# Retention attention with a gated feed-forward layer: moving the v loads from GpSimd's queue to the hardware queues, with the first tiles put in a new order

## The chip, the cores and the metric

The kernel runs on one core of one Trainium2 chip. The metric is the device time of one execution in microseconds; the kernel before takes 238.09 us (median of 3 runs, 238.08 to 238.14). The profiled execution took 238.38 us, of which 236.7 us lie between its first and its last instruction; times inside the profile are counted from that first instruction.

## The reference, cut to what matters

Attention with a decaying state (batch 4, 8 heads, 768 positions, 64 numbers per head), then a feed-forward layer on 3072 tokens with 512 features and 1536 hidden units:

```python
gamma = 1.0 - 2.0 ** (-5.0 - np.arange(H))
for t in range(S):                       # the state decays by gamma, then takes k v^T
    state = gamma * state + einsum('bhd,bhe->bhde', k[:, :, t], v[:, :, t])
    y[:, :, t] = scale * einsum('bhd,bhde->bhe', q[:, :, t], state)
x = y.transpose(0, 2, 1, 3).reshape(B * S, H * D)
gate = 1 / (1 + exp(-(x @ w_gate)))
out = (gate * (x @ w_val)) @ w_out
```

## The kernel before, where the change touches it

The 3072 tokens are cut into 24 chunks of 128 (index `g`) and into 6 token tiles of 512 (index `t`, four chunks each). For a chunk the kernel loads k, q and v. k and q are turned into bf16 during the transfer[...]; v stays in 32 bits, and it too is issued by GpSimd, except that of chunk 0.

```python
def load_v(g, eng):
    vf[g] = ld.tile([C, H, D], F32, tag="vf", name="vf", bufs=8)
    eng.dma_start(out=vf[g], in_=src(v, g))

def load_kq(g):                       # k and q of a chunk, cast to bf16 on the way
    ...
    nc.gpsimd.dma_start(out=kn[g], in_=src(k, g))
    nc.gpsimd.dma_start(out=qn[g], in_=src(q, g))

def load_chunk(g):
    load_kq(g)
    load_v(g, nc.gpsimd)
```

The steps of one chunk: `transposes(g)` turns k and q on TensorE and ScalarE copies them out (`qkT`); from chunk 12 on a DMA transpose does it. `scale_v` multiplies v by the decay table into `vs`. `scores` makes k q^T, `masks` applies the causal mask on VectorE. `inter` adds the part of the output that comes from the state, `state` adds k v^T to the state, `intra` the part from inside the chunk, `state_out` copies the state out on ScalarE, and `y_out` multiplies by the table `taby` on VectorE into `xT`, the input of the feed-forward layer.

The feed-forward layer of a token tile is 12 groups `up(t, n1)` (gate and value, 8 matmuls; ScalarE applies the sigmoid, VectorE multiplies) and 8 half groups `down` (6 matmuls each; after every second one ScalarE copies the result out). The three weights are loaded by GpSimd in pieces: six of gate and of value (`load_gate_val`, two `n1` each) and four of the output weight (`load_out`, three `n1` each).

The start, before the loop over the tiles. `keep_on(n)` issues n matmuls whose result nobody uses; they fill TensorE's waits:

```python
    scale_v(0, nc.gpsimd)
    load_gate_val(0)
    scale_v(1, nc.gpsimd)
    load_chunk(3)
    load_gate_val(1)
    load_gate_val(2)
    ...                               # chunk 0's k and q cast on VectorE and ScalarE
    keep_on(36)
    transposes(0)
    make_taby(slice(256, 384))
    extend_taby()                     # GpSimd: taby[384:768] from taby[0:384]
    for s in range(3, NFF // 2):
        load_gate_val(s)
    load_chunk(4)
    for s in range(4):
        load_out(s)
    for g in range(5, 8):
        load_chunk(g)
    ...                               # chunks 0, 1 and 2, with keep_on between
    intra(2)
    y_out(2)
    scale_v(3, nc.vector)
    keep_on(8)
    up(0, 0, 0, 384)                  # the columns of chunks 0 to 2 only
    up(0, 1, 0, 384)
    transposes(3)
    scores(3)
    masks(3)
    inter(3); state(3); state_out(3)
    up(0, 2, 0, 384)
    intra(3)
    y_out(3)
    up(0, 3, 0, 384)
    up_columns(0, range(4), 384, 512) # chunk 3's columns of the first four groups
```

In the loop the steps of the next tile's chunks are put between the groups. For tile 0 they are:

```python
        if t == 0:
            groups = groups[4:]
            steps = [lambda: step_t(4), lambda: step_s(4), lambda: step_y(4), lambda: step_t(5), lambda: step_s(5),
                     lambda: step_t(6), lambda: step_y(5, 6), lambda: step_t(7), lambda: step_y(6, 7)]
            place = [4, 5, 7, 9, 10, 11, 12, 13, 14]
```

`step_t` is transposes and `scale_v`; `step_s` scores and masks; `step_y(g, n)` is inter, scores of chunk n, state, intra, masks of n and `y_out`. Chunk 7's last step comes in tile 1, after the first group there.

Of the kernel before, what the change touches and what calls it, by code (L numbers as in the profile page):

```python
# [9 lines left out]
F32 = mybir.dt.float32  # L10
BF16 = mybir.dt.bfloat16
I32 = mybir.dt.int32
AX = mybir.ActivationFunctionType
ALU = mybir.AluOpType
# [3 lines left out]
def kernel(  # L18
# [10 lines left out]
    nc = tc.nc  # L29
# [28 lines left out]
        return x[b, :, c * C:(c + 1) * C, :].rearrange("h s d -> s h d")  # L58

    def load_v(g, eng):  # L60
        vf[g] = ld.tile([C, H, D], F32, tag="vf", name="vf", bufs=8)
        eng.dma_start(out=vf[g], in_=src(v, g))  # L62

    def load_kq(g):
        kn[g] = ld.tile([C, H, D], BF16, tag="kn", name="kn")
        qn[g] = ld.tile([C, H, D], BF16, tag="qn", name="qn")
        nc.gpsimd.dma_start(out=kn[g], in_=src(k, g))  # L67
        nc.gpsimd.dma_start(out=qn[g], in_=src(q, g))  # L68

    def load_chunk(g):  # L70
        load_kq(g)
        load_v(g, nc.gpsimd)

    wg = wpool.tile([128, KT, D_FF], BF16, name="wg")
    wv = wpool.tile([128, KT, D_FF], BF16, name="wv")
# [2 lines left out]
    def load_gate_val(s):  # L78
        cols = slice(s * 256, (s + 1) * 256)
        for dst, w in ((wg, moe_w_gate), (wv, moe_w_val)):  # L80
            nc.gpsimd.dma_start(out=dst[:, :, cols],  # L81
                                in_=w.rearrange("(kk p) n -> p kk n", p=128)[:, :, cols])

    def load_out(s):
# [7 lines left out]
    nc.sync.dma_start(out=qf, in_=src(q, 0))  # L92
    nc.scalar.preload_act_table(AX.Exp)
    load_v(0, nc.sync)
    tokv = const.tile([128, NCH], I32, name="tokv")
    nc.gpsimd.iota(tokv, pattern=[[C, NCH]], base=0, channel_multiplier=1)
    ident = const.tile([128, 128], BF16, name="ident")
    make_identity(nc, ident)
    toky = const.tile([128, 384], I32, name="toky")
    nc.gpsimd.iota(toky, pattern=[[1, 384]], base=0, channel_multiplier=0)  # L100
    load_chunk(1)
    causal = const.tile([128, 128], F32, name="causal")
    nc.gpsimd.memset(causal, 1.0)
    nc.gpsimd.affine_select(causal, causal, pattern=[[1, 128]], base=0, channel_multiplier=-1,
                            compare_op=ALU.is_ge, fill=0.0)
    load_chunk(2)

    tabv = const.tile([128, NCH, H], F32, name="tabv")
    for h in range(H):
# [16 lines left out]
        for p in range(NP):  # L126
            nc.scalar.activation(taby[:, p, cols], toky[:, cols], AX.Exp, scale=lgp[:, p:p + 1], bias=lsc)

    def extend_taby():
        nc.gpsimd.tensor_tensor(taby[:, :, 384:768], taby[:, :, 0:384],  # L130
                                gup.unsqueeze(2).to_broadcast([128, NP, 384]), op=ALU.mult)

    causal4 = causal.unsqueeze(1).to_broadcast([128, NP, 128])

# [7 lines left out]
    def transposes(g):  # L142
        tp = pa.tile([128, 2 * NP, C], BF16, tag="tp", name="tp")
        for i, x in enumerate((kn[g], qn[g])):
            for p in range(NP):
                nc.tensor.transpose(tp[:, i * NP + p, :], pair(x, p), ident)  # L146
        qkT[g] = at.tile([128, 2 * NP, C], BF16, tag="qkT", name="qkT", bufs=3)
        nc.scalar.activation(qkT[g], tp, AX.Copy)  # L148
# [7 lines left out]
    def scale_v(g, eng):  # L156
        vs[g] = ld.tile([C, H, D], BF16, tag="vs", name="vs", bufs=4)
        eng.tensor_tensor(vs[g], vf[g], tabv[:, g % NCH, :].unsqueeze(2).to_broadcast([C, H, D]),  # L158
                          op=ALU.mult)
# [16 lines left out]
    def inter(g):  # L176
        y[g] = pa.tile([128, NP, C], F32, tag="y", name="y")
        if g % NCH > 0:
            for p in range(NP):
                nc.tensor.matmul(y[g][:, p, :], zbd[(g - 1) % 2][:, p, :], qkT[g][:, NP + p, :],  # L180
                                 start=(p == 0), stop=False, skip_group_check=True)

    def state(g):
        b, c = divmod(g, NCH)
        if c == 0:
            zps[b] = pa.tile([128, NP, D], F32, tag="z", name="z", padded_shape=[128, NP, C])
        if c < NCH - 1:
            for p in range(NP):
                for i in range(2):
                    nc.tensor.matmul(zps[b][i * D:(i + 1) * D, p, :], kn[g][:, 2 * p + i, :], vs[g][:, 2 * p + i, :],  # L190
                                     start=(c == 0 and p == 0), stop=True, skip_group_check=True)

    def state_out(g):
        b, c = divmod(g, NCH)
        if c < NCH - 1:
            for i in range(2):
                half = slice(i * D, (i + 1) * D)
                nc.scalar.copy(zbd[g % 2][half, :, half], zps[b][half])  # L198
# [8 lines left out]
    def y_out(g):  # L207
        c = g % NCH
        if g % 4 == 0:
            xT[g // 4] = at.tile([128, NP, 512], BF16, tag="xT", name="xT")  # L210
        col = (g % 4) * C
        nc.vector.tensor_tensor(xT[g // 4][:, :, col:col + C], y[g], taby[:, :, c * C:(c + 1) * C], op=ALU.mult)  # L212

    def step_t(g):
        if g < XBAR:
            transposes(g)
        scale_v(g, nc.vector if g < XBAR else nc.gpsimd)

    def step_s(g):
        scores(g)  # L220
        masks(g)

    def step_y(g, nxt=None):
        inter(g)
        if nxt is not None:
            scores(nxt)
        state(g)
        intra(g)
        state_out(g)
        if nxt is not None:  # L230
            masks(nxt)
        y_out(g)
# [10 lines left out]
    def up(t, n1, lo=0, hi=512):  # L243
        if t not in hT:
            hT[t] = ffn.tile([128, NFF, 512], BF16, tag="hT", name="hT", bufs=2)
        ps = []
        for w in (wg, wv):
            u = pf.tile([128, 512], F32, tag="ff", name="ff")
            for kk in range(KT):
                nc.tensor.matmul(u[:, lo:hi], w[:, kk, n1 * 128:(n1 + 1) * 128], xT[t][:, kk, lo:hi],  # L250
                                 start=(kk == 0), stop=(kk == KT - 1))
            ps.append(u)
        gs = ffn.tile([128, 512], F32, tag="gs", name="gs")
        nc.scalar.activation(gs[:, lo:hi], ps[0][:, lo:hi], AX.Sigmoid)  # L254
        nc.vector.tensor_tensor(hT[t][:, n1, lo:hi], gs[:, lo:hi], ps[1][:, lo:hi], op=ALU.mult)  # L255
# [34 lines left out]
    def keep_on(n):  # L290
        u = pf.tile([128, 512], F32, tag="ff", name="ff")
        for _ in range(n):
            nc.tensor.matmul(u[:, :128], ident, ident, start=True, stop=True)  # L293
# [18 lines left out]
                eng.dma_start(out=out[row:row + 128, first:first + 128], in_=ob)  # L312


    scale_v(0, nc.gpsimd)
    load_gate_val(0)
    scale_v(1, nc.gpsimd)
    load_chunk(3)
    load_gate_val(1)
    load_gate_val(2)  # L320
    make_taby(slice(0, 256))
    kn[0] = ld.tile([C, H, D], BF16, tag="kn", name="kn")
    qn[0] = ld.tile([C, H, D], BF16, tag="qn", name="qn")
    nc.vector.tensor_copy(kn[0], kf)
    nc.scalar.copy(qn[0], qf)
    keep_on(36)
    transposes(0)
    make_taby(slice(256, 384))
    extend_taby()
    for s in range(3, NFF // 2):  # L330
        load_gate_val(s)
    load_chunk(4)
    for s in range(4):
        load_out(s)
    for g in range(5, 8):
        load_chunk(g)
    keep_on(8)
    scores(0)
    masks(0)
    keep_on(8)  # L340
    transposes(1)
    inter(0)
    state(0)
    state_out(0)
    intra(0)
    y_out(0)
    keep_on(8)
    scores(1)
    masks(1)
    keep_on(4)  # L350
    inter(1)
    state(1)
    state_out(1)
    transposes(2)
    nc.scalar.preload_act_table(AX.Sigmoid)
    intra(1)
    y_out(1)
    scale_v(2, nc.vector)
    keep_on(12)
    scores(2)  # L360
    masks(2)
    inter(2)
    state(2)
    state_out(2)
    keep_on(10)
    intra(2)
    y_out(2)
    scale_v(3, nc.vector)
    keep_on(8)
    up(0, 0, 0, 384)  # L370
    up(0, 1, 0, 384)
    transposes(3)
    scores(3)
    masks(3)
    inter(3)
    state(3)
    state_out(3)
    up(0, 2, 0, 384)
    intra(3)
    y_out(3)  # L380
    up(0, 3, 0, 384)
    up_columns(0, range(4), 384, 512)


    def ups(t):
# [5 lines left out]
    for t in range(NT):  # L391
        groups, steps, place = ups(t) + downs(t), [], []
        if t == NT - 1:
            groups[-2:] = [lambda: last_down(t)]
        if t == 0:
            groups = groups[4:]
            steps = [lambda: step_t(4), lambda: step_s(4), lambda: step_y(4), lambda: step_t(5), lambda: step_s(5),
                     lambda: step_t(6), lambda: step_y(5, 6), lambda: step_t(7), lambda: step_y(6, 7)]
            place = [4, 5, 7, 9, 10, 11, 12, 13, 14]
        elif t + 1 < NT:  # L400
            steps = attention(t + 1)
            place = [0, 1, 3, 5, 7, 8, 10, 13, 17]
        if t == 1:
            groups[:2] = [lambda: up(1, 0, 0, 384), lambda: step_y(7), lambda: up(1, 1, 0, 384),
                          lambda: up_columns(1, range(2), 384, 512)]
            place = [p + 2 for p in place]
        if t + 2 < NT:
            for g in range(4 * t + 8, 4 * t + 12):
                load_chunk(g)
        for i, group in enumerate(groups):  # L410
            if i == len(groups) - 9:
                for g in range(4 * t + 8, 4 * t + 12):
                    if XBAR <= g < NG:
                        xbar(g)
            group()
            for p, step in zip(place, steps):
                if p == i:
                    step()
# [30 lines left out]
```

## Time and profile before

| | value |
|---|---|
| device time, median | 238.09 us |
| span in the profile | 236.7 us |
| granted TensorE clock | 0.997 |
| TensorE busy | 227.0 us (96%) |
| VectorE / ScalarE / GpSimd busy | 105.4 / 90.7 / 91.9 us |
| q0, filled by GpSimd: packets, bytes | 57616, 16.78 MB |
| q1, filled by SyncE: packets, bytes | 19776, 10.10 MB |
| v loads from GpSimd | 23 of 256 KB |

Matmuls overlap one another in the records, so the time between two starts says more than the length of one. A row of the timeline gives start, length, engine, line, operation and tiles, and in square brackets how long the engine had been idle and what it had waited for. "Landing" of a DMA is the time from its issue to the semaphore that tells of its data. A list of DMA issues of a short stretch of time gives the landing of single loads.

### The profile page before, as it was taken

The numbers are of one execution on the slowest core, as the hardware profiler recorded it, in microseconds if no ns is written. First come the engines' busy times: TensorE is split into PE (matmuls) and PEld (weight loads), VectorE is DVE, ScalarE is ACT, GpSimd is POOL, SyncE is SP. The second block draws the span as 40 slices with busy tenths as digits, with TensorE's granted clock in tenths as the row PEclk, the third lists the DMA queues.
The fourth block names the chain that finished last, engine by engine and source line by source line (L and its number), as shares of the span: only waits on it lengthen the run. The fifth ranks groups of instructions, "written<-read, shape, count | busy, mean of one in ns | idle before, by whom it ended". The sixth has DMA issues, their size and how long they took to land.

```text
span 236.7 us, 4316 instructions
## 1 busy us (share of the span) xinstructions
PE 227.0 (96%) x1712; PEld 119.5 (51%) x1738; DVE 105.4 (45%) x178; ACT 90.7 (38%) x170; POOL 91.9 (39%) x110
## 2 busy tenths in 40 slices
PE   7888999999999999999999999999999999999994
PEld 7665644555555554444554445444444554444443
DVE  3468446365646741346641256641346641234300
ACT  8765334425545431344333343233334331333211
POOL 8999875686787244985311001111000000000000
PEclk9999999999999999999999999999999999999998
DMA  7999999999999999999972442012100012100022
GB/s 121 196 191 181 189 203 205 191 206 233 223 182 132 127 146 157 273 143 166 164 118 89 92 89 44 3 46 90 47 0 0 3 44 87 46 3 0 0 89 89
DMA packets 77699, 27.27 MB, mean 115 GB/s; under 512 B 65072, under 2 KB 73264, under 8 KB 77680
## 3 DMA queue, kind: packets, MB, share of 16 engines
q0 software_dynamic: 57616, 16.78, 70.6%
q1 hardware_dynamic: 19776, 10.10, 21.0%
q8 instruction: 13, 0.21, 0.4%
q10 hardware_dynamic: 288, 0.13, 0.2%
q14 instruction: 6, 0.05, 0.1%
HBM read 28.31 MB, written 6.29 MB: 146 GB/s over the span
## 4 chain that ended last, share of the span: by engine, by line
PE 90%; DMA 3%; ACT 2%; POOL 2%; issue 1%; DVE 1%; SPq 0%; ACTq 0%; DVEq 0%; POOLq 0%
PE ff L250 51%; PE ff L281 25%; PE sA L168 3%; DMA vf<-in_v_dram 3%; PE y L204 2%; PE y L180 2%; PE z L190 2%; PE tp L146 2%; ACT qkT L148 1%; PE ff L301 1%; POOL vs L158 1%; PE ff L264 1%; DVE xT L212 1%; ACT ob L286 1%; POOL wg L81 0%
## 5 line engine op out<-in xcount | busy, mean ns | idle before, releaser
L255 DVE TENSOR_TENSOR hT<-gs,ff 128x512 bf16<-128x512 f32 (+1 forms) x72 | 48.6, 676 | 73.6 <-PE ff L250 70.7
L250 PE MATMUL ff<-xT,wg 128*128 128x512 bf16 (+1 forms) x276 | 71.5, 375 | 0.9 <-DVE xT L212 0.3
L250 PE MATMUL ff<-xT,wv 128*128 128x512 bf16 (+1 forms) x282 | 71.8, 375 | 0.4
L254 ACT ACTIVATE gs<-ff 128x512 f32<-128x512 f32 (+1 forms) x72 | 42.3, 588 | 68.8 <-PE ff L250 68.3
L281 PE MATMUL ff<-wo,hT 128*128 128x512 bf16 x268 | 62.4, 379 | 0.6 <-issue 0.2
L250 PEld LDWEIGHTS <-wv 128*128 128x128 bf16 x288 | 28.2, 98 | 32.7
L250 PEld LDWEIGHTS <-wg 128*128 128x128 bf16 x288 | 26.6, 98 | 30.2 <-issue 0.8
L281 PEld LDWEIGHTS <-hT 128*128 128x128 bf16 x276 | 25.9, 98 | 30.2
L286 ACT COPY ob<-ff 128x512 f32<-128x512 f32 x23 | 13.5, 585 | 52.3 <-PE ff L281 47.0
L158 POOL TENSOR_TENSOR vs<-vf,tabv 128x512 bf16<-128x512 f32 x14 | 14.5, 1046 | 44.7 <-PE y L204 39.5
L62 POOL DMA_DIRECT2D vf<-in_v_dram x23 | 20.7, 899 | 13.8 <-DMA kn<-in_k_dram 5.7
L212 DVE TENSOR_TENSOR xT<-y,taby 128x512 bf16<-128x512 f32 x24 | 16.4, 684 | 20.3 <-PE y L204 20.2
L173 DVE TENSOR_TENSOR stA<-sA,causal 128x512 bf16<-128x512 f32 x24 | 16.5, 687 | 17.3 <-PE sB L168 17.2
L67 POOL DMA_DIRECT2D kn<-in_k_dram x23 | 20.7, 901 | 8.4 <-PE ff L250 4.3
L68 POOL DMA_DIRECT2D qn<-in_q_dram x23 | 20.4, 887 | 3.9 <-DMA wo<-in_moe_w_out_dram 2.2
L198 ACT CAST zbd<-z 64x256 bf16<-64x256 f32 x40 | 14.6, 366 | 12.7 <-PE z L190 12.4
L174 DVE TENSOR_TENSOR stB<-sB,causal 128x512 bf16<-128x512 f32 x24 | 16.3, 680 | 0.0
L148 ACT ACTIVATE qkT<-tp 128x1024 bf16<-128x1024 bf16 x12 | 12.3, 1024 | 5.4 <-PE tp L146 5.3
L158 DVE TENSOR_TENSOR vs<-vf,tabv 128x512 bf16<-128x512 f32 x10 | 8.9, 894 | 3.1 <-DMA vf<-in_v_dram 3.1
L293 PE MATMUL ff<-ident 128*128 128x128 bf16 x94 | 8.7, 260 | 1.6 <-POOL ident masks.py:199 1.6
L204 PE MATMUL y<-stA,vs 128*64 128x128 bf16 x96 | 9.7, 222 | 0.0
L204 PE MATMUL y<-stB,vs 128*64 128x128 bf16 x96 | 9.5, 221 | 0.0
(52 smaller groups left out, 121.1 us busy)
## 6 DMA issues: line engine op xcount, KB each, us to landing
vf<-in_v_dram POOLq DMA_DIRECT2D x23, 256.0 KB, 9.2
out_dram<-ob SPq DMA_DIRECT2D x23, 256.0 KB, 2.0
kn<-in_k_dram POOLq DMA_DIRECT2D x23, 128.0 KB, 9.4
qn<-in_q_dram POOLq DMA_DIRECT2D x23, 128.0 KB, 9.6
wg<-in_moe_w_gate_dram POOLq DMA_DIRECT2D x6, 256.0 KB, 6.0
wv<-in_moe_w_val_dram POOLq DMA_DIRECT2D x6, 256.0 KB, 6.6
wo<-in_moe_w_out_dram POOLq DMA_DIRECT2D x4, 384.0 KB, 10.4
kf<-in_k_dram SPq DMA_DIRECT2D x1, 256.0 KB, 3.5
```

The source lines that it names most:

```text
L62: eng.dma_start(out=vf[g], in_=src(v, g))
L67: nc.gpsimd.dma_start(out=kn[g], in_=src(k, g))
L68: nc.gpsimd.dma_start(out=qn[g], in_=src(q, g))
L158: eng.tensor_tensor(vs[g], vf[g], tabv[:, g % NCH, :].unsqueeze(2).to_broadcast([C, H, D]), op=ALU.mult)
L173: nc.vector.tensor_tensor(stA[g], sc[g][0], causal4, op=ALU.mult)
L174: nc.vector.tensor_tensor(stB[g], sc[g][1], causal4, op=ALU.mult)
L204: nc.tensor.matmul(y[g][i * D:(i + 1) * D, p, :], vs[g][:, 2 * p + i, :], st[:, p, :], start=(first and p == 0), stop=True, skip_group_che ...
L212: nc.vector.tensor_tensor(xT[g // 4][:, :, col:col + C], y[g], taby[:, :, c * C:(c + 1) * C], op=ALU.mult)
L250: nc.tensor.matmul(u[:, lo:hi], w[:, kk, n1 * 128:(n1 + 1) * 128], xT[t][:, kk, lo:hi], start=(kk == 0), stop=(kk == KT - 1))
L254: nc.scalar.activation(gs[:, lo:hi], ps[0][:, lo:hi], AX.Sigmoid)
L255: nc.vector.tensor_tensor(hT[t][:, n1, lo:hi], gs[:, lo:hi], ps[1][:, lo:hi], op=ALU.mult)
L281: nc.tensor.matmul(o, hT[t][:, n1, sm * 128:(sm + 1) * 128], wo[:, n1, :], start=(n1 == 0), stop=(n1 == NFF - 1))
```

## The change

All v loads but the first two (now on SyncE's queue at the start) are issued from ScalarE's queue, three chunks ahead of their use, inside `step_t`; the v buffers go from 8 to 5. GpSimd then issues only k, q and the weights, so the weights stand nearer the front of its queue. The first tiles get a new order: all weights go ahead of k and q of chunk 4; the table is extended in two pieces; chunk 3's transposes come before the first `up`; `up_columns` takes three groups, not four; the fillers are fewer; and the steps of chunks 4 to 7 move behind all `up` groups of tile 0, into its `down` half.

```diff
-        vf[g] = ld.tile([C, H, D], F32, tag="vf", name="vf", bufs=8)
+        vf[g] = ld.tile([C, H, D], F32, tag="vf", name="vf", bufs=5)
...
-    def load_chunk(g):
-        load_kq(g)
-        load_v(g, nc.gpsimd)
...
     load_v(0, nc.sync)
+    load_v(1, nc.sync)
...
-    load_chunk(1)
+    load_kq(1)
...
-    load_chunk(2)
+    load_kq(2)
...
-    def extend_taby():
-        nc.gpsimd.tensor_tensor(taby[:, :, 384:768], taby[:, :, 0:384],
+    def extend_taby(lo, hi):
+        nc.gpsimd.tensor_tensor(taby[:, :, lo:hi], taby[:, :, lo - 384:hi - 384],
...
         if g < XBAR:
             transposes(g)
+        if g + 3 < NG:
+            load_v(g + 3, nc.scalar)
         scale_v(g, nc.vector if g < XBAR else nc.gpsimd)
...
+    load_gate_val(0)
     scale_v(0, nc.gpsimd)
-    load_gate_val(0)
     scale_v(1, nc.gpsimd)
-    load_chunk(3)
-    load_gate_val(1)
-    load_gate_val(2)
+    load_kq(3)
...
+    load_v(2, nc.scalar)
+    scale_v(2, nc.gpsimd)
+    extend_taby(384, 512)
+    for s in range(1, NFF // 2):
+        load_gate_val(s)
     keep_on(36)
     transposes(0)
     make_taby(slice(256, 384))
-    extend_taby()
-    for s in range(3, NFF // 2):
-        load_gate_val(s)
-    load_chunk(4)
+    extend_taby(512, 768)
     for s in range(4):
         load_out(s)
-    for g in range(5, 8):
-        load_chunk(g)
+    for g in range(4, 8):
+        load_kq(g)
...                                   (fillers 8+8+8+4+12+10+8 become 8+6+4+6+12)
     transposes(1)
+    load_v(3, nc.scalar)
...
+    load_v(4, nc.scalar)
     nc.scalar.preload_act_table(AX.Sigmoid)
...
     y_out(2)
+    transposes(3)
     scale_v(3, nc.vector)
-    keep_on(8)
+    load_v(5, nc.scalar)
     up(0, 0, 0, 384)
-    up(0, 1, 0, 384)
-    transposes(3)
     scores(3)
     masks(3)
     inter(3)
     state(3)
     state_out(3)
-    up(0, 2, 0, 384)
+    up(0, 1, 0, 384)
     intra(3)
     y_out(3)
-    up(0, 3, 0, 384)
-    up_columns(0, range(4), 384, 512)
+    load_v(6, nc.scalar)
+    up(0, 2, 0, 384)
+    up_columns(0, range(3), 384, 512)
...
-            groups = groups[4:]
-            steps = [lambda: step_t(4), lambda: step_s(4), lambda: step_y(4), lambda: step_t(5), lambda: step_s(5),
-                     lambda: step_t(6), lambda: step_y(5, 6), lambda: step_t(7), lambda: step_y(6, 7)]
-            place = [4, 5, 7, 9, 10, 11, 12, 13, 14]
+            groups = groups[3:]
+            steps = attention(1)[:-1]
+            place = [10, 11, 12, 13, 13, 14, 14, 15]
...
             for g in range(4 * t + 8, 4 * t + 12):
-                load_chunk(g)
+                load_kq(g)
```

More of the change, by code (lines that the diff above doesn't have):

```diff
@@ L127, in make_taby @@
             nc.scalar.activation(taby[:, p, cols], toky[:, cols], AX.Exp, scale=lgp[:, p:p + 1], bias=lsc)
-    def extend_taby():
-        nc.gpsimd.tensor_tensor(taby[:, :, 384:768], taby[:, :, 0:384],
-                                gup.unsqueeze(2).to_broadcast([128, NP, 384]), op=ALU.mult)
+    def extend_taby(lo, hi):
+        nc.gpsimd.tensor_tensor(taby[:, :, lo:hi], taby[:, :, lo - 384:hi - 384],
+                                gup.unsqueeze(2).to_broadcast([128, NP, hi - lo]), op=ALU.mult)
     causal4 = causal.unsqueeze(1).to_broadcast([128, NP, 128])
@@ L339 @@
     masks(0)
-    keep_on(8)
+    keep_on(6)
     transposes(1)
+    load_v(3, nc.scalar)
     inter(0)
@@ L346 @@
     y_out(0)
-    keep_on(8)
+    keep_on(4)
     scores(1)
     masks(1)
-    keep_on(4)
+    transposes(2)
     inter(1)
     state(1)
+    keep_on(6)
     state_out(1)
-    transposes(2)
-    nc.scalar.preload_act_table(AX.Sigmoid)
     intra(1)
     y_out(1)
-    scale_v(2, nc.vector)
-    keep_on(12)
+    load_v(4, nc.scalar)
+    nc.scalar.preload_act_table(AX.Sigmoid)
     scores(2)
@@ L364 @@
     state_out(2)
-    keep_on(10)
+    keep_on(12)
     intra(2)
     y_out(2)
+    transposes(3)
     scale_v(3, nc.vector)
-    keep_on(8)
+    load_v(5, nc.scalar)
     up(0, 0, 0, 384)
-    up(0, 1, 0, 384)
-    transposes(3)
     scores(3)
```

## The prediction, made before the changed kernel ran

> **What bounds the kernel now.** I read the page's engine shares first, then the chain of waits, then TensorE's timeline of the first 55 us, then DMA: stretches of time and the landings of single loads.
>
> ```profile
> PE 227.0 (96%) x1712; PEld 119.5 (51%) x1738; DVE 105.4 (45%) x178; ACT 90.7 (38%) x170; POOL 91.9 (39%) x110
> PE   7888999999999999999999999999999999999994
> DMA  7999999999999999999972442012100012100022
> PE 90%; DMA 3%; ACT 2%; POOL 2%; issue 1%; DVE 1%; SPq 0%; ACTq 0%; DVEq 0%; POOLq 0%
> ```
>
> TensorE is busy 227.0 of 236.7 us and makes 90% of the chain that ended last; only in the first four slices (24 us) does it have room. The DMA row shows a second thing: the 16 DMA engines are full for the first 20 slices, about 118 us. So a change of the load queues can win only near the start, and there it meets full DMA engines.
>
> TensorE's timeline (start, length, instruction, idle before):
>
> ```profile
> 17.26 0.81 PE L250 MATMUL ff<-xT,wg 128*128 128x384 bf16 x4 [0.30 <-DVE xT L212]
> ...
> 19.85 0.39 PE L146 MATMUL tp<-ident,kn 128*128 128x128 bf16 x4
> 20.08 0.39 PE L146 MATMUL tp<-ident,qn 128*128 128x128 bf16 x4
> 21.58 0.23 PE L168 MATMUL sA<-qkT 64*128 64x128 bf16 x1 [1.12 <-ACT qkT L148]
> ```
>
> The first `up` starts at 17.26. From there to the last matmul the row has one hole of note, the 1.12 us at 21.58: chunk 3's scores wait for ScalarE's copy of its transposes. Busy time by stretch (PE, PEld, DVE, ACT, POOL, clock, DMA share, GB/s) agrees: nearly 12 of 12 us in the two later ones.
>
> ```profile
> 18.00:30.00 12.00, 10.83 (x109) 6.96 (x109) 8.08 (x10) 4.91 (x9) 11.00 (x13) 1.00 1.39 185
> 30.00:42.00 12.00, 11.95 (x68) 5.61 (x68) 5.93 (x10) 5.09 (x8) 7.62 (x9) 1.00 1.46 203
> 42.00:54.00 12.00, 11.89 (x110) 6.61 (x111) 6.38 (x10) 4.62 (x8) 9.49 (x11) 1.00 1.84 199
> ```
>
> The DMA rate hardly moves (185 to 203 GB/s) and the share is over 1 throughout: no stretch in which a transfer could be had for nothing.
>
> **Landings, from the lists of issues of short stretches.** Issue time plus time to landing: k of chunk 3 11.90 + 4.3 = 16.2, q 12.84 + 4.3 = 17.1, v 13.71 + 4.4 = 18.1. So a small load costs the full engines about 0.95 us. Pieces of gate and value land at 20.0, 21.3, 22.8, 24.5, 25.6, 26.9, 28.3, 29.6, 31.0 and 32.4: about 1.4 us each. Chunk 4's k, q, v follow at 33.3, 34.3, 35.2; the four pieces of the output weight at 36.8, 38.7, 40.6, 42.6 (1.9 each); then chunk 5's k, q, v at 43.5, 44.6, 45.8 and chunk 7's at 49.7, 50.5, 51.5. Against that, TensorE transposes chunk 5 at 45.42 and chunk 7 at 52.93. The kernel before is laid out just behind its transfers.
>
> [...] SyncE's v of chunk 0, among GpSimd's k and q, took 6.3 us to land, while SyncE's first load took 3.5. [...]
>
> ```profile
> 17.54 2.83 POOL L130 TENSOR_TENSOR taby<-taby,gup 128x1536 f32<-128x1536 f32 x1
> ...
> 18.14 2.79 DVE L158 TENSOR_TENSOR vs<-vf,tabv 128x512 bf16<-128x512 f32 x1 [0.93 <-DMA vf<-in_v_dram]
> ```
>
> (0.68 us is what this VectorE multiply takes elsewhere.) [...] SyncE's three loads held it 0.46, 0.56 and 1.08 us, so I take 0.5 to 1 us of ScalarE for each v load[...].
>
> **The change part by part.**
>
> *GpSimd.* 22 v issues leave it (chunk 1's goes to SyncE), 22 x 0.9 = 20 us of 92. The chain gives GpSimd 2%, most of it vs of chunk 1 (1.08 us at 10.91, ahead of z); that one still waits for v. Gain on the path: about 0.
>
> *ScalarE.* 22 issues x 0.5 to 1 us = 11 to 22 us on an engine with 38% busy. In the `up` phase a group lasts 1.73 us; sigmoid 0.60 leaves 1.1, and the transposes' copy (1.02) falls in the same group only for chunks 8 to 11, where 0.1 to 0.3 us may be lost per chunk. Up to +0.5 us, I take +0.2.
>
> *The start.* To chunk 3's v, fourteen small loads and two weight pieces have landed by 18.1 in the kernel before. The changed one asks for the same set in the same time; only the order differs. v of chunks 1 to 3 now goes beside k and q, not behind, and the first weight pieces stand ahead of k and q of chunk 3. So q of chunk 1 lands later (9.05 before, I estimate 10.4), and q of chunk 3, now the last of the set, lands at about 18.1, not 17.1. The transposes of chunk 3 stand ahead of the first `up` in TensorE's order, so that starts at 18.1 + 0.45 + a little = 18.7, which is +1.4 us.
>
> *After it.* The 1.12 us hole goes, since the first `up` (1.30 us) covers the copy: -1.1. The transposes (0.45) are done already: -0.45. The fillers cost nothing in either kernel where TensorE waits anyway.
>
> *Tile 0's `up` groups.* The kernel before takes 17.26 to 42.82 = 25.56 us from the first `up` to the first `down`. Less the hole 1.12, the transposes 0.45 and chunk 4's steps, which move behind (transposes 0.44, scores 0.33, the rest 0.79 = 1.56), that is 22.4. So the first `down` could start at 18.7 + 22.4 = 41.1. Its output weight had landed by 36.8 to 42.6 with fifteen small loads ahead of it; now it is two (k and q of chunk 0), seven v (0 to 6) and six k and q (1 to 3): fifteen again. The last piece is used some 2 us into the phase, at 43, so this just fits.
>
> *Chunk 4's transposes.* Two `down` halves (12 x 0.216 = 2.6 us) later, at 43.7, TensorE asks for q of chunk 4. Ahead of it now stand all weights and seventeen small loads (k and q of 0 to 4, v of 0 to 6). In the kernel before, the eighteenth (v of chunk 5) landed at 45.8 with the same weights. So I expect 45.8 - 1.0 = 44.8: a new wait of about 1.1 us, on DMA. From there to chunk 7's transposes it is three transposes (1.32), scores of chunk 4 (0.33), two steps of 1.12 and four `down` halves of 1.30 = 9.1, so 53.9, where the kernel before has 52.93 with the same work done by then.
>
> The sum at that point: +1.4 - 1.1 - 0.45 + 1.1 = +0.95 us, and with ScalarE's 0.2 about +1.1. Later nothing of size changes: from 60 to 140 us TensorE is busy 79.2 of 80.
>
> **The rivals.** *First: the retiming pays.* If loads on two rows overlap better than those on one, or if q of chunk 3 gets ahead of v, then the first `up` starts near 17 and chunk 4's k and q are there at 43: no new waits, the hole and 0.45 gone, some 0.3 more from fillers. That makes about 236.5. For it: the counts of fillers and the new places look chosen for this timing. Against it: the rate over all early stretches is 185 to 203 GB/s whatever the queue. *Second: ScalarE becomes a brake.* If an issue holds it 1.5 us or more, the chain transposes, copy, scores is longer for eight early chunks, and psum tiles come free late: +2 to +4, so 240 to 242. For it: 1.08 us for the third load in a row. Against it: three of four issues of one queue are far apart here. *Third: hidden anyway.* The wait for chunk 4's q hides whatever the start gains or loses, so 238.3 to 239 whether the first `up` is at 17.5 or at 19. This is close to my own case: only the arrival at 44.8 matters.
>
> **Range and chances.** The working says 239.2, the first rival 236.5. I give the working two thirds of the weight and the first rival a bit under a third: 2/3 x 239.2 + 1/3 x 236.5 = 238.3, with the second rival's tail 238.5. The range 236.8 to 240.2 leaves out the better ends of the first and most of the second. A change of 2% is 4.8 us; TensorE's whole room before its dense part is hardly more, so faster 0.02; slower by that needs ScalarE held up in most chunks: 0.03; within 2%: 0.95.
>
> **What would show it.** The first `up` at 18 to 19 with the transposes of chunk 3 waiting for q by DMA; no wait on `qkT` behind the first `up`; a wait of about 1 us by DMA at chunk 4's transposes, near 44.8; chunk 7's transposes at 53 to 54; DMA as full as before to beyond 90 us, at the same GB/s; ScalarE's v issues at 0.5 to 1 us. I am wrong if TensorE gets k and q of chunk 4 without a wait and the first `up` is at 17 or earlier (then the first rival), or if holes of over 0.3 us recur behind 55 us with ScalarE named (then the second).

## The result, and the profile after

The changed kernel takes 253.81 us (median of 4 runs, 252.57 to 254.81), against 238.09 before: a ratio of 1.0657, 95% interval 1.0609 to 1.0706. It is slower by 15.7 us, and the prediction, 238.5 us with a range of 236.8 to 240.2, was wrong. The profiled span is 252.2 us, 15.5 more than before. Line numbers shift by a few between kernels; the names of the tiles are the same.

The page of the kernel after, in the same lines as those shown of the kernel before, with the row of the granted TensorE clock added:

```profile
PE 228.8 (91%) x1682; PEld 118.6 (47%) x1708; DVE 102.4 (41%) x177; ACT 90.8 (36%) x170; POOL 73.0 (29%) x89
PE   7589999899307999999999999999999999999994
PEclk9979999999855999999999999999999999999999
DMA  8999999999999951129992258511230002200022
PE 67%; DMA 25%; POOL 4%; issue 1%; SPq 1%; ACT 1%; ACTq 0%; DVE 0%; POOLq 0%
```

One slice is 6.3 us. TensorE's row now has a gap, 3 and 0 tenths in slices 11 and 12 (counted from 1), about 63 to 76 us, and the clock row shows the granted clock falling to about half in it and behind it (8, 5 and 5 tenths in slices 11 to 13). In the chain that ended last, DMA has gone from 3% to 25%. All this lies in the stretch that the prediction passed over with one sentence.

TensorE's timeline of the kernel after, around that gap and at its end:

```profile
64.23 1.04 PE L249 MATMUL ff<-xT,wg 128*128 128x512 bf16 x3
77.09 1.87 PE L249 MATMUL ff<-xT,wv 128*128 128x512 bf16 x4 [11.81 <-ACT gs L268]
78.75 1.91 PE L249 MATMUL ff<-xT,wg 128*128 128x512 bf16 x4
...
82.03 1.03 PE L249 MATMUL ff<-xT,wg 128*128 128x512 bf16 x4
82.89 1.03 PE L249 MATMUL ff<-xT,wv 128*128 128x512 bf16 x4
```

TensorE stands still for 11.81 us, and what releases it is a sigmoid on ScalarE (`gs`): until that has read the result of an earlier group, none of the three `ff` buffers is free for TensorE's next results. After it, four matmuls take 1.66 us from start to start (77.09 to 78.75), twice the 0.86 of those at 82.03.

So what held ScalarE? Its timeline in the kernel after ("ACTq" is an issue of a DMA by ScalarE's sequencer):

```profile
62.83 1.02 ACT L145 ACTIVATE qkT<-tp 128x1024 bf16<-128x1024 bf16 x1 [0.61 <-PE tp L143]
76.21 0.40 ACTq L62 DMA_DIRECT2D vf<-in_v_dram  x1
76.65 0.38 ACT L268 ACTIVATE gs<-ff 128x256 f32<-128x256 f32 x1 [12.80 <-DMA qkX<-kn]
```

After the copy of chunk 8's transposes ScalarE does nothing until 76.21; then it issues the v load of chunk 11, and only then comes the sigmoid, 12.80 us late. The trace puts the wait down to a DMA transpose (`qkX<-kn`, chunk 12's k) that neither the sigmoid nor this v load uses. The issue itself is short, 0.40 us: in the trace the 12.80 us are idle time of ScalarE, not a long issue. So the length of an issue, from which the prediction took its cost, does not tell of the wait ahead of it.

The chain that ended last, in the kernel after (start, length, what):

```profile
55.58 13.34 DMA kn<-in_k_dram
...
68.94 7.17 DMA qkX<-kn
...
76.21 0.40 ACTq L62
...
76.65 0.39 ACT gs L268
...
77.09 4.66 PE ff L249 x12
```

k of chunk 12 is issued at 55.58 and needs 13.34 us; the DMA transpose of it is issued at 68.94 and lands 7.17 us later, at 76.11; 0.10 us after that landing ScalarE issues v of chunk 11; then comes the sigmoid; then TensorE. I call this theory A: ScalarE's v load stands until the first of SyncE's transposes has landed, and its own buffer has no part in it. The two share no data and are issued by different engines, and what ties them together the trace does not show; that the next v load would stand in the same way if this one went out earlier was an assumption of mine. Rival B, that running transposes hold up the issue, does not fit these times: ScalarE is idle from 63.85, the first transpose is issued only at 68.94, and the v load goes out at 76.21 while another transpose is being issued (76.05 to 78.33).

The start, in TensorE's timeline of the kernel after:

```profile
18.80 0.40 PE L143 MATMUL tp<-ident,qn 128*128 128x128 bf16 x4 [0.50 <-DMA qn<-in_q_dram]
19.03 0.81 PE L249 MATMUL ff<-xT,wg 128*128 128x384 bf16 x4
...
43.78 0.81 PE L280 MATMUL ff<-wo,hT 128*128 128x512 bf16 x3 [0.40 <-DMA wo<-in_moe_w_out_dram]
45.70 0.40 PE L143 MATMUL tp<-ident,qn 128*128 128x128 bf16 x4 [0.56 <-DMA qn<-in_q_dram]
...
54.56 0.40 PE L143 MATMUL tp<-ident,kn 128*128 128x128 bf16 x4
...
58.78 0.81 PE L249 MATMUL ff<-xT,wg 128*128 128x384 bf16 x4
```

The last row is the first group of tile 1; the kernel before has it at 57.14. So the 15.5 us of span are 58.78 - 57.14 = 1.64 in the first tile, the hole of 11.81, and some 1.9 of slow clock behind it (twelve matmuls from 77.09 to 81.58, where the next instruction starts; at full clock they take 12 x 0.216 = 2.6): 15.35.

### The profile page after: what moved, and what is told of

Read it like the earlier page. It is cut to its first block, busy times and chain, and to the rows that moved or that the text cites. A ratio compares the mean times of both kernels' runs of the same rounds, so it can differ in the third digit from the quotient of the medians.

```text
span 252.2 us, 4268 instructions
## 1 busy us (share of the span) xinstructions
PE 228.8 (91%) x1682; PEld 118.6 (47%) x1708; DVE 102.4 (41%) x177; ACT 90.8 (36%) x170; POOL 73.0 (29%) x89
## 3 DMA queue, kind: packets, MB, share of 16 engines
q10 hardware_dynamic: 23168, 5.90, 13.1%
## 4 chain that ended last, share of the span: by engine, by line
PE 67%; DMA 25%; POOL 4%; issue 1%; SPq 1%; ACT 1%; ACTq 0%; DVE 0%; POOLq 0%
PE ff L249 40%; PE ff L280 20%; DMA wo<-in_moe_w_out_dram 5%; DMA kn<-in_k_dram 5%; DMA wv<-in_moe_w_val_dram 5%; DMA qn<-in_q_dram 4%; DMA qkX<-kn 3%; DMA vf<-in_v_dram 2%; PE sA L165 2%; PE y L201 2%; PE y L177 1%; PE z L187 1%; PE ff L300 1%; POOL wg L77 1%; POOL vs L155 1%
## 5 line engine op out<-in xcount | busy, mean ns | idle before, releaser
L249 PE MATMUL ff<-xT,wv 128*128 128x512 bf16 (+1 forms) x282 | 73.1, 380 | 12.2 <-ACT gs L268 11.8
L249 PE MATMUL ff<-xT,wg 128*128 128x512 bf16 (+1 forms) x276 | 72.6, 379 | 0.6
L155 POOL TENSOR_TENSOR vs<-vf,tabv 128x512 bf16<-128x512 f32 x15 | 15.9, 1058 | 91.5 <-DMA vf<-in_v_dram 38.6
L68 POOL DMA_DIRECT2D qn<-in_q_dram x23 | 20.4, 888 | 10.5 <-DMA qn<-in_q_dram 7.9
L292 PE MATMUL ff<-ident 128*128 128x128 bf16 x72 | 7.2, 274 | 1.6 <-POOL ident masks.py:199 1.6
L177 PEld LDWEIGHTS <-zbd 128*128 128x128 bf16 x80 | 6.2, 100 | 4.4 <-issue 0.4
L143 PE MATMUL tp<-ident,qn 128*128 128x128 bf16 x48 | 4.9, 227 | 3.0 <-DMA qn<-in_q_dram 3.0
```

## The experiments

The table gives the median time, and the ratio to the kernel before with its 95% interval. Two of the 20 executions of run 5 (241.97 and 242.28 us) and three of the 22 of run 12 (241.53 to 245.67 us) were more than 1.5% slower than the fastest; they are in the median but not in the ratio. The diffs of 1, 2, 3, 5 and 11 are against the kernel after, those of 4 and 7 against the kernel before, the others against the run that they name.

| | what it is | us | ratio |
|---|---|---|---|
| 1 | after, v with eight buffers | 252.68 | 1.0610 (1.0589 to 1.0631) |
| 2 | after, v of chunk 11 one step earlier | 249.72 | 1.0486 (1.0464 to 1.0508) |
| 3 | after, the loop's v on SyncE | 240.72 | 1.0112 (1.0095 to 1.0129) |
| 4 | before, with the new v queues only | 253.82 | 1.0658 (1.0631 to 1.0686) |
| 5 | before, with the new order only | 238.52 | 1.0008 (0.9992 to 1.0024) |
| 6 | 3, with more fillers | 241.24 | 1.0135 (1.0102 to 1.0168) |
| 7 | before, chunk 3's transposes ahead | 237.93 | 0.9985 (0.9967 to 1.0004) |
| 8 | 7, v from chunk 7 on SyncE | 242.29 | 1.0174 (1.0159 to 1.0189) |
| 9 | 5, v from chunk 7 on SyncE | 242.97 | 1.0206 (1.0193 to 1.0219) |
| 10 | 7, chunk 3's k and q ahead of weights | 239.81 | 1.0093 (1.0071 to 1.0115) |
| 11 | after, chunks 12 to 15 transposed by TensorE | 243.29 | 1.0203 (1.0171 to 1.0234) |
| 12 | 5, vs of chunk 0 ahead of weights | 238.89 | 1.0030 (1.0013 to 1.0047) |

### 1. Eight buffers for v

```diff
-        vf[g] = ld.tile([C, H, D], F32, tag="vf", name="vf", bufs=5)
+        vf[g] = ld.tile([C, H, D], F32, tag="vf", name="vf", bufs=8)
```

> The changed kernel with 8 v buffers in place of 5. Theory A [...]: ScalarE's issue of v of chunk 11 stands still [...]. Buffers have no part in it: the 11 to 12 us hole of TensorE at 64 to 77 us stays, time 252 to 255. Rival C (too few v buffers: chunk 11's load waits for chunk 6's buffer): the hole is gone, time about 239 to 241.

ScalarE's timeline:

```profile
74.52 0.38 ACTq L62 DMA_DIRECT2D vf<-in_v_dram  x1
74.99 0.39 ACT L268 ACTIVATE gs<-ff 128x256 f32<-128x256 f32 x1 [11.14 <-DMA qkX<-kn]
```

The hole stays, at 11.14 us on ScalarE and 10.2 on TensorE, and the trace names the same DMA transpose. The first of them is issued at 67.70 here, and the load goes out 6.82 us behind it, in the kernel after 7.27 us. Rival C, too few buffers, falls.

### 2. v of chunk 11 issued a step earlier

```diff
-        if g + 3 < NG:
+        if g + 3 < NG and g != 8:
             load_v(g + 3, nc.scalar)
+        if g == 7:
+            load_v(11, nc.scalar)
```

> The changed kernel with v of chunk 11 issued by ScalarE one step earlier, beside that of chunk 10, ahead of the transposes [...]. Theory A: chunk 11's issue no longer waits, but [...] now chunk 12's v, issued in chunk 9's step at about 69 us, [...] waits until that lands at about 76: a shorter hole of 5 to 7 us at about 70 us, time 245 to 249. Rival B [...]: the hole should shrink in the same way only if the issue stood behind running transposes; it would then start no earlier than 69 us and be at most one transpose (2 us) long, time 240 to 243. Rival C: as the changed kernel or worse, 253 and up.

ScalarE's timeline:

```profile
77.27 0.38 ACTq L62 DMA_DIRECT2D vf<-in_v_dram  x1
77.75 1.09 ACT L255 ACTIVATE gs<-ff 128x512 f32<-128x512 f32 x2 [7.10 <-DMA qkX<-kn]
```

v of chunk 11 is now issued in time (its issue and that of v of chunk 10 lie between 56.64 and 59.87); the next one, of chunk 12, is issued at 77.27, 6.92 us behind the first transpose (70.35), and stands still in its place. The hole shrinks to 6.2 us on TensorE and moves to the next v load. The time, 249.72, is a little above what theory A gave, and far above the 240 to 243 of rival B.

### 3. The same loads, issued by SyncE

```diff
         if g + 3 < NG:
-            load_v(g + 3, nc.scalar)
+            load_v(g + 3, nc.sync)
```

> The changed kernel with the v loads inside step_t issued by SyncE in place of ScalarE; the five at the start stay on ScalarE. Theory A: [...] an issue that stands still holds only SyncE, which computes nothing: the hole is gone, and what is left is the cost of the first 55 us, 1.7 to 2.2 us over the kernel before: 239.5 to 240.5. If the hole came from DMA bandwidth or from late v data, it would stay: 250 and up.

The queue of SyncE in this run:

```profile
60.05 9.88 SPq L62 DMA_DIRECT2D vf<-in_v_dram  x4
70.28 3.17 SPq L150 DMA_TRANSPOSE qkX<-kn  x1
```

Neither ScalarE nor TensorE has a hole now, and the span is 238.6 us. It is not the old wait on another engine, as I had expected: SyncE issues v of chunks 11 to 14 ahead of the transposes, so none of these four can wait for one. Their issues spread over 9.88 us, and I take it that they wait for a buffer: v of chunk 14 needs that of chunk 9, and in run 8, with the same four loads, VectorE has read v of chunk 9 at 71.34 and the last issue ends at 71.73. The transposes stand behind them to 70.28; but that holds SyncE alone, and TensorE waits for none of it. This one word takes back 13.1 of the 15.7 us; the time is 0.2 us above the range that theory A gave. What is left, 2.6 us, is the subject of most of the other runs.

### 4 and 5. The two halves of the change, each alone

4: the order of the kernel before, v on SyncE and ScalarE as in the kernel after (chunks 1 to 6 at about the same places, then in `step_t`, five buffers).

```diff
     def load_chunk(g):
         load_kq(g)
-        load_v(g, nc.gpsimd)
+    load_v(1, nc.sync)
...
+        if g + 3 < NG:
+            load_v(g + 3, nc.scalar)
...
+    load_v(2, nc.scalar)                 (likewise 3 to 6)
```

> The kernel before with the load queues of the change alone (v on SyncE and ScalarE, three chunks ahead, 5 buffers), but the old order of weights, tables, first tiles and steps. Theory A: [...] the hole comes with the queues and not with the retiming: ScalarE stands from about 62 us to the first transpose's landing, some 8 to 13 us; time 247 to 253. If the hole comes from the retiming (k of chunk 12 late), it is gone: 238 to 240.

5: the order of the kernel after, all v but the first by GpSimd with `load_chunk`, eight buffers.

```diff
-        if g + 3 < NG:
-            load_v(g + 3, nc.scalar)
...
-    load_kq(1)
+    load_chunk(1)                        (likewise 2 to 23)
```

> The changed kernel's order (weights ahead, first tiles, steps of chunks 4 to 7 behind the up groups) with every v but chunk 0's issued by GpSimd as before, 8 buffers. Theory A [...]: no hole behind 60 us. Theory D (v beside k and q is what makes q of chunks 1 to 3 late): with v behind them in one queue q of chunk 1 lands near 9 us and q of chunk 3 near 17, the first up starts at 17.5 to 18.3 in place of 19.0, and there is no half-clock stretch; the wait for chunk 4's q at 44 to 45 stays, as it comes from the order of weights ahead: 238.3 to 239.3. Rival (the retiming alone costs what is left): as with v on SyncE, 240 to 241.

ScalarE's timeline of 4:

```profile
74.77 0.39 ACTq L62 DMA_DIRECT2D vf<-in_v_dram  x1
75.21 0.38 ACT L271 ACTIVATE gs<-ff 128x256 f32<-128x256 f32 x1 [8.31 <-DMA qkX<-kn]
```

The load goes out 7.03 us behind the first transpose (67.74). The hole goes with the queues and not with the order, which alone makes no difference that can be measured (238.52). That 4 takes as long as both together (253.82 us) is chance: its hole is shorter, 7.3 us on TensorE in place of 11.81, and its start is longer. TensorE waits 3.45 us at 18.59 for vs, and the first group of tile 1 comes at 61.78, 4.64 us later than in the kernel before, where with the new order it is 1.64.

In 5 the wait for chunk 4's q that I expected at 44 to 45 us did not come (the row at 43.54). TensorE's timeline of 5:

```profile
10.70 0.32 PE L190 MATMUL z<-vs,kn 128*64 128x64 bf16 x8 [1.57 <-POOL vs L158]
...
18.37 0.81 PE L250 MATMUL ff<-xT,wg 128*128 128x384 bf16 x4 [0.30 <-DVE xT L212]
...
43.54 0.40 PE L146 MATMUL tp<-ident,qn 128*128 128x128 bf16 x4
...
52.41 0.40 PE L146 MATMUL tp<-ident,kn 128*128 128x128 bf16 x4
```

Chunk 7's transposes come at 52.41. TensorE's timeline of run 3 has them later:

```profile
54.84 0.40 PE L143 MATMUL tp<-ident,kn 128*128 128x128 bf16 x4
```

The two differ only in the queues and the buffers of v (five in 3, eight in 5), and the 2.43 us between them are about the difference of their times (240.72 - 238.52 = 2.2). In 5 the v of chunks 4 to 6 stand behind q of chunk 4 in GpSimd's one queue; in 3 they are issued earlier, on other queues, and are carried before it. I read this as the cost of the v loads at the start: not their issue, but their place ahead of k and q.

### 6. Fillers against the slow clock at the start

The kernel after shows a granted clock of 0.72 between 12 and 18 us, and run 3 has a 7 in its clock row. Theory E puts part of the 2.6 us down to it. Edit to run 3: the fillers ahead of the transposes of chunks 1, 2 and 3 become 28, 18 and 26 matmuls.

```diff
-    keep_on(6)
+    keep_on(28)
     transposes(1)
...
+    keep_on(18)
     transposes(2)
...
+    keep_on(26)
     transposes(3)
```

> The kernel with v of the loop on SyncE, and more fillers at TensorE's three waits for k and q at the start (28 in place of 6 before chunk 1's transposes, 18 before chunk 2's, 26 before chunk 3's), so that TensorE isn't idle there. Theory E (part of the 2.6 us over the kernel before is half clock, granted after these idle stretches): the granted clock stays at 1.00 and the time falls by 0.5 to 1.3 us from 240.7 to 239.4 to 240.2. Rival (only the late transfers count, and chunk 4's q hides the rest): same as without, 240.4 to 241.

TensorE's timeline of run 6, at chunk 4's q:

```profile
45.88 0.40 PE L143 MATMUL tp<-ident,qn 128*128 128x128 bf16 x4 [0.57 <-DMA qn<-in_q_dram]
```

The same row in TensorE's timeline of run 3:

```profile
45.98 0.40 PE L143 MATMUL tp<-ident,qn 128*128 128x128 bf16 x4 [0.32 <-DMA qn<-in_q_dram]
```

The clock is full throughout (9 tenths or more in every slice), and nothing comes of it (241.24): what TensorE gains earlier it waits for q of chunk 4, which comes at 45.9 either way. Theory E falls for the start: the low clock is there (the 7 in run 3's row), but hidden behind the next transfer.

### 7. The kernel before, with chunk 3's transposes ahead of the first `up`

```diff
     scale_v(3, nc.vector)
-    keep_on(8)
+    transposes(3)                        (ahead of scale_v)
     up(0, 0, 0, 384)
     up(0, 1, 0, 384)
-    transposes(3)
```

> The kernel before, with one thing of the change alone: chunk 3's transposes ahead of the first up in place of eight fillers. Both theories: the 1.12 us wait of chunk 3's scores for the copy goes; q of chunk 3 lands at 17.1, so the first up starts at about 17.6 in place of 17.26, and the transposes are done: about 1.1 us less, 236.8 to 237.4. If chunk 5's transfers (q at 44.6, v at 45.8 against its transposes at 45.4) are a wall, half of that is given back: 237.3 to 238.

TensorE's timeline:

```profile
16.49 0.40 PE L146 MATMUL tp<-ident,kn 128*128 128x128 bf16 x4 [0.36 <-DMA kn<-in_k_dram]
17.39 0.40 PE L146 MATMUL tp<-ident,qn 128*128 128x128 bf16 x4 [0.51 <-DMA qn<-in_q_dram]
...
22.39 0.82 PE L250 MATMUL ff<-xT,wv 128*128 128x384 bf16 x4 [0.34 <-DMA wv<-in_moe_w_val_dram]
```

The hole of 1.12 us is gone, and three waits on DMA (1.21 us together) have taken its place. 237.93 us: the same within the interval, in the second of the two ranges and not the first. The loss is at chunk 3's k and q and one piece of value, though, not at chunk 5's transfers. In the trace some 0.6 us of the gain are kept: the first group of tile 1 starts at 56.52, in the kernel before at 57.14.

### 8 and 9. v on SyncE from chunk 7 only

8 is run 7, with v of chunks 4 to 6 on ScalarE and of 7 to 23 on SyncE. 9 is run 5, with v of 1 to 6 left to GpSimd and of 7 to 23 on SyncE. Both have five buffers.

```diff
+        if g + 3 < NG:
+            load_v(g + 3, nc.sync)
```

> The same, with v of chunks 4 to 6 on ScalarE and of chunks 7 to 23 on SyncE, three ahead, 5 buffers; v of chunks 1 to 3 stays with GpSimd. Theory A: no hole behind 60 us, since an issue that stands still holds only SyncE. GpSimd's k and q of chunks 5 to 7 land earlier and v later, no sum of bytes changes: the same as the run before it within 0.4 us. If DMA sets the pace near 45 us, it's up to 0.5 us better; if SyncE's loads that stand still make the transposes of chunks 12 to 15 or the v of chunks 11 to 14 late, it is 1 to 3 us worse.

> The retiming with v of chunks 1 to 6 from GpSimd, behind k, q and weights, and only v of chunks 7 to 23 from SyncE, three ahead, 5 buffers. Theory D (what is left over the kernel before, 2.6 us in the run with the loop's v on SyncE, comes from v of chunks 1 to 6, which on hardware queues go beside k, q and weights [...]): no waits for q of chunks 1, 3 and 4 beyond those of the retiming alone, time 238.2 to 239.2. Rival (v of the loop on SyncE costs it): 240 to 241.

SyncE's queue in run 8 (the first of the two is v of chunk 0, the second v of chunk 7, at the end of the 12.77 us):

```profile
1.94 12.77 SPq L62 DMA_DIRECT2D vf<-in_v_dram  x2
```

TensorE's timeline of run 8:

```profile
19.12 0.40 PE L146 MATMUL tp<-ident,qn 128*128 128x128 bf16 x4 [1.71 <-DMA qn<-in_q_dram]
...
38.89 0.40 PE L146 MATMUL tp<-ident,kn 128*128 128x128 bf16 x4 [1.88 <-DMA kn<-in_k_dram]
```

TensorE's timeline of run 9:

```profile
53.65 0.40 PE L146 MATMUL tp<-ident,kn 128*128 128x128 bf16 x4 [1.10 <-DMA kn<-in_k_dram]
56.67 0.40 PE L146 MATMUL tp<-ident,qn 128*128 128x128 bf16 x4 [2.62 <-DMA qn<-in_q_dram]
```

Both are slower than expected (9 slower even than its rival gave), and the traces point to one reason. In 8, v of chunk 7 goes out near 14 us, although the source has it in chunk 4's step: nothing else holds SyncE back, so it is sent as soon as its buffer is free (VectorE has read v of chunk 2 at 14.32, and the issue ends at 14.71), while q of chunk 3 is on its way. ScalarE issues v of chunk 4 at 12.69, so two v loads stand beside that q. In 9 chunk 4 has no wait, as theory D said, but the v loads on SyncE from 44.6 on now make k and q of chunk 7 late (1.10 + 2.62 us). So theory D in its first form, that only the v of chunks 1 to 6 do harm, falls. The wider form fits 3, 5, 8 and 9: while the DMA engines are full (9 tenths or more in the first 16 slices of run 9, some 96 us), a v load on a queue of its own takes its share at once, and the k and q that TensorE needs next come later.

For 9 the trace has that share. GpSimd has issued the same loads up to q of chunk 7 as in 5, and issues that q at the same time, 45.04 in 5 and 45.09 in 9. The list of DMA issues of 5 around 45.05 (the last number is the time to landing):

```profile
qn<-in_q_dram POOLq DMA_DIRECT2D x1, 128.0 KB, 7.6
```

The list of DMA issues of 9 around 45.1:

```profile
qn<-in_q_dram POOLq DMA_DIRECT2D x1, 128.0 KB, 11.5
```

From 45 to 57 us GpSimd's queue moves 1.88 MB in 5 and 1.18 in 9; SyncE's, which carries the output too, moves 0.72 and 1.08.

### 10. Chunk 3's k and q ahead of the first weights

Run 7, with chunk 3's k and q ahead of the first weight pieces on GpSimd.

```diff
+    load_kq(3)
     load_gate_val(0)
     scale_v(1, nc.gpsimd)
-    load_chunk(3)
+    load_v(3, nc.gpsimd)
```

> The kernel before with chunk 3's transposes ahead of the first up, and k and q of chunk 3 loaded ahead of the first pieces of gate and value (v of chunk 3 behind them). If the waits for that k and q (0.36 and 0.51 us in the run without this) are what kept the moved transposes from paying, the first up starts at about 17.0 and the time is 236.8 to 237.4. If the weights then come late instead (second piece of value at 21.3 or later, needed at about 21.5), it is the same as without, 237.5 to 238.1.

TensorE's timeline:

```profile
13.41 0.32 PE L190 MATMUL z<-vs,kn 128*64 128x64 bf16 x8 [1.91 <-POOL vs L158]
```

The waits for chunk 3's k and q are gone, but GpSimd, which computes vs of chunk 1 behind these issues, is late by two issues (about 0.9 us each), and the first `up` starts at 20.20, not at about 17.0. The time rises to 239.81, above both ranges. What this shares with theory A is that an issue delays what stands behind it on the engine that issues.

### 11. No DMA transposes for chunks 12 to 15

```diff
-    XBAR = 12
+    XBAR = 16
```

> The changed kernel with v left on ScalarE, but chunks 12 to 15 turned by TensorE like those before them, so that no DMA transposes are issued between 60 and 77 us; scale_v of these four goes to VectorE with it. Theory A [...]: no idle time of ScalarE over 1 us that ends on a DMA transpose, no hole of TensorE near 64 to 77 us, full clock there; 239.8 to 240.7 us as with the loop's v on SyncE plus 4 x 0.45 us of transposes, so 241.5 to 243 us. Rival F (ScalarE's issues as such, or v's own transfer among full DMA engines, make the hole): idle time of 5 us or more stays in front of a sigmoid between 60 and 80 us, whatever ends it, and the time stays over 248 us.

ScalarE's timeline:

```profile
63.91 1.02 ACT L145 ACTIVATE qkT<-tp 128x1024 bf16<-128x1024 bf16 x1 [0.61 <-PE tp L143]
63.97 0.37 ACTq L62 DMA_DIRECT2D vf<-in_v_dram  x1
64.83 0.38 ACT L268 ACTIVATE gs<-ff 128x256 f32<-128x256 f32 x1
```

With v still on ScalarE, v of chunk 11 is issued at once, the sigmoid follows at 64.83, and the hole is gone. 243.29 us, 0.3 above the range that theory A gave; the hole and its slow clock are worth 10.5 us net of the four chunks' transposes on TensorE. Rival F, ScalarE's issues as such, falls.

### 12. The new order, with vs of chunk 0 early

Run 5 without its wait of 1.57 us at 10.70: `scale_v(0)` again ahead of the first weight issues.

```diff
+    scale_v(0, nc.gpsimd)
     load_gate_val(0)
-    scale_v(0, nc.gpsimd)
     scale_v(1, nc.gpsimd)
```

> The retiming with v by GpSimd and eight buffers, as in the run that did this alone, but scale_v of chunk 0 stands ahead of the first two weight issues on GpSimd again, as in the kernel before. In that earlier run z of chunk 0 waited 1.57 us for it, behind 1.56 us of issues. If that wait is worth its length: z at 9.2 instead of 10.7, first up 17.0 to 17.5, chunk 4 still without a wait, 237.0 to 237.7 us, a version that beats both kernels. If the arrival of chunk 3's q (17.3 in the run with transposes(3) moved alone) or of the weights sets the first groups anyway: a wait on DMA or on wv appears between 16.5 and 23 us, and the time is 237.8 to 238.6 us, the same as before.

TensorE's timeline:

```profile
17.55 0.40 PE L146 MATMUL tp<-ident,qn 128*128 128x128 bf16 x4 [0.25 <-DMA qn<-in_q_dram]
17.83 0.81 PE L250 MATMUL ff<-xT,wg 128*128 128x384 bf16 x4
...
43.99 0.40 PE L146 MATMUL tp<-ident,qn 128*128 128x128 bf16 x4 [0.62 <-DMA qn<-in_q_dram]
```

The first `up` comes 0.54 us earlier than in 5 (17.83 against 18.37), and TensorE then waits 0.62 us for q of chunk 4. 238.89 us, 0.3% above the kernel before and a little above the second range: no version here beats the kernel before by more than its interval.

## Why the prediction was wrong

The step that failed is the end of the change part by part: "Later nothing of size changes: from 60 to 140 us TensorE is busy 79.2 of 80", and with it the second rival, "ScalarE becomes a brake", which I sized by how long an issue holds ScalarE. It holds it 0.37 to 0.43 us, less than the 0.5 to 1 us that I took. What I left out is that an issue can wait, and that on ScalarE everything behind it then waits too. One issue of 22 did; it held ScalarE for 12.80 us and cost 13.7 us (11.81 of hole, 1.9 of slow clock). Runs 1, 2, 3 and 11 settle that it waited for the first DMA transpose: not for a buffer (1); let the load go a step earlier and the next one waits (2); take the transposes away and nothing waits (11); put the loads on SyncE, where they go out ahead of the transposes, and none waits for a transpose, while those that wait for a buffer hold an engine that computes nothing (3). Why a load of ScalarE has to wait for that landing, they do not show.

The row I leant on was the wrong one for the question. TensorE busy 79.2 of 80 us says that nothing is amiss in that stretch of the kernel before; it says nothing of what a new instruction in ScalarE's order would wait for. For the wait that came, the kernel before has at least the earliest time. SyncE's queue there, at its first DMA transpose:

```profile
67.21 1.30 SPq L153 DMA_TRANSPOSE qkX<-kn  x1
```

TensorE transposes chunk 8 at 60.53 there, and the new load stands right behind that. If it has to wait for this transpose to land, it cannot go out before 67.21.

The prediction gave a sign for its second rival, holes over 0.3 us behind 55 us with ScalarE named. Such a hole came, but the rival's cause, long issues, did not.

The other steps, one by one:

- *GpSimd is relieved, with no gain on the path*: right. It is busy 73.0 instead of 91.9 us, near the 20 us less that were predicted, and the early waits are for data, not for GpSimd.
- *The start*: right in mechanism. q of chunk 3 is used at 18.80 and the first `up` starts at 19.03, predicted 18.1 and 18.7. That q is issued at 11.06, 1.8 us earlier than before, and takes 7.7 us to land in place of 4.3: loads on other queues go beside it. The count in the working is off: k, q and v of chunks 0 to 3 are twelve small loads, not fourteen, and v of chunk 4, issued at 14.16 while this q was under way, is not among them.
- *After it*: the 1.12 us hole went, as predicted. Whether that is worth 1.1 us depends on what comes next: in run 7, which takes only the hole out of the kernel before, waits for data take its place.
- *Chunk 4's wait*: right, and 0.9 us later than predicted: q at 45.70, not 44.8, with a wait of 0.56 us on it and 0.40 on the output weight. With the order alone (run 5) this wait does not come; it fits the v loads of chunks 4 to 6 ahead of q, as the count of seventeen small loads in the prediction had it.
- *The sum of the first tile*: +0.95 predicted at chunk 7's transposes (53.9 against 52.93), +1.63 measured there (54.56) and +1.64 at the first group of tile 1. Run 3, which has just this and no hole, takes 240.72 us, so without the failed step the prediction would still have been about 2 us low, just outside its range.
- *The rival "hidden anyway"*: right for the new order. By the first `down` run 6 is 1.24 us ahead of run 3 (41.43 against 42.67) and run 12 0.47 ahead of run 5 (40.13 against 40.60), and both give it back at q of chunk 4. In run 7, which keeps the old order, some 0.6 us stay in the trace.

Run 3's profiled span is only 1.9 us longer than that of the kernel before (238.6 - 236.7), not 2.6, because of the executions that were profiled: 240.32 us against run 3's median of 240.72, and 238.38 against 238.09.

What stays open: the wider form of theory D fits four runs, but the share of each queue is compared only between 5 and 9; for 3 and 8 it is argued. What makes a v load of ScalarE wait for a transpose of SyncE is not shown. The place of the loads was changed for one of them (run 2) and for all together with the engine (run 3); a version that keeps v on ScalarE and the DMA transposes, with all these loads issued in time, was not tried. So the 13.1 us of run 3 are not split between the place and the engine.

## What to carry to other kernels

Before a load goes to another engine, list what its issue may wait for, not only how long it lasts: a buffer, or a landing, here that of another engine's transfer (12.80 us of wait for an issue of 0.40). On ScalarE everything behind it waited as well; on SyncE, which computes nothing, four v issues spread over 9.88 us left no hole in TensorE (run 3). So of these two SyncE was the place for loads that may wait (240.72 us against 253.81). But it keeps no pace with the computation: in run 8 it issued v of chunk 7 as soon as its buffer was free, at about 14 us, while the DMA engines were full, and TensorE then waited 1.71 us for the q that it needed next, where in run 7 it waited 0.51. Here one queue in order of need did what a second queue beside it did not (238.5 us in run 5 against 240.7 in run 3), and a wait shortened early was waited again at the next landing (runs 6 and 12).

## What the runs showed of the hardware that was not expected

- A v load whose issue takes 0.40 us held ScalarE idle for 12.80 us until another engine's DMA transpose, with which it shares no data, had landed. In the four runs with such a hole (the kernel after, 1, 2 and 4) the load went out 6.82 to 7.27 us behind the issue of the first transpose.
- An issue by ScalarE took 0.37 to 0.43 us even with the DMA engines full; SyncE's first three took 0.46 to 1.08 in the kernel before. Beside a DMA transpose it was not longer either (0.40 at 76.21); the transpose's own issue was, 2.28 us against 1.2 to 1.6 for the other seven.
- After 11.81 us of idleness TensorE ran at half clock for about 4 us (0.415 us a matmul, then 0.216). The clock was also low (0.72) from 12 to 18 us, and 0.50 in each us from 13 to 16, where no single wait since 5 us was longer than 1.15 us; so only short waits came before it there. In stretches of time of the kernel after (PE, PEld, DVE, ACT and POOL busy, then clock, DMA share, GB/s):

```profile
63.00:78.00 15.00, 2.91 (x27) 1.50 (x26) 1.54 (x4) 1.72 (x3) 11.37 (x13) 0.64 2.17 151
78.00:83.00 5.00, 5.00 (x24) 2.24 (x23) 2.52 (x5) 1.37 (x2) 0.00 (x0) 0.70 1.66 165
```

  In the last row TensorE is busy all of the 5 us, and slow: a busy share alone would not show it.
